# Spectrum rows for the second half of the partitions: copied once within HBM, then read with one load per chunk

## The chip, the cores and the metric

The kernel runs on one core of a Trainium2 chip. The metric is the device time of one execution in microseconds (us); lower is better. A profile of one more execution shows what each engine did: TensorE (PE, with its weight loads as PEld), VectorE (DVE), ScalarE (ACT), GpSimd (POOL), SyncE (SP, which only issues transfers here), and the DMA engines. "L418" means line 418 of the kernel.

## What is computed

A long convolution along the sequence by FFT, then a token-mixing layer on its result:

```python
# x: (8, 5696, 128), h: (5696, 128)
Yf = rfft(x, n=2*S, axis=1) * rfft(h, n=2*S, axis=0)[None]
y  = irfft(Yf, n=2*S, axis=1)[:, :S, :]
theta = y @ w_theta
u   = y + w_tok_r @ (y * cos(theta)) + w_tok_i @ (y * sin(theta))   # over the sequence
out = u + relu(u @ w_ch)
```

The change touches only the first two lines.

## The kernel before

The convolution takes the first 361 us or so, the mixing nearly all the rest. The transform of length 2 x 5696 is done as two factors, 178 x 64. The 8 sequences and 128 channels are handled in eight groups, each of two sequences and 64 channels (`groups`, L493; `dh` is the half of the channels). A group goes through four stages.

- **Stage A** (`stage_a`, L241): 16 chunks of four matmuls (L250), evicted from PSUM to the tile `a` by ScalarE or VectorE (L257, L259).
- **Stage B** (`stage_b`, L400): 12 chunks of up to eight frequencies (`NCK` is 12). TensorE forms the spectrum of x (`f2`, L262, matmuls L270; after the last chunk `warm` extra matmuls L276), ScalarE copies it out of PSUM as `xs` (L416), and VectorE multiplies it by the spectrum of h (L418; L423 for the short last chunk). The product needs both the real and the imaginary rows of h's spectrum, and on the upper 64 partitions those two exchanged. They lie in HBM as `hf_hbm`, and `load` (L404) brings a chunk into the tile `hs` with two transfers, one for partitions 0 to 63 (L408) and one, with the order of the pair reversed, for partitions 64 to 127 (L409). `hs` has four buffers (`LEAD`): a chunk's load is issued four chunks ahead, when the product of an earlier chunk has released its buffer.
- **Stage C** (`stage_c`, L429): the inverse's first half, 16 chunks of 16 matmuls (L438, L439) into a PSUM tile, evicted to the tile `g` (L443 by ScalarE, L445 by VectorE). In all groups but the last, ScalarE takes the chunks with q % 32 == 24, that is chunks 3, 7, 11 and 15.
- **Stage D** (`stage_d`, L463): the inverse's second half, seven chunks of matmuls (L474) with the table `e_t` of cosines and sines, and with `e_neg`, a negated copy of some of its rows (`e_minus`, L397), evicted to `yt` (L478, L480), which is stored to `yt_hbm` (L487).

`woven` (L280) writes two or more lists of such steps interleaved by given positions. The loop over groups (L762 to L788) writes stage C of group g woven with stage A of group g + 1, the first four spectrum loads of group g + 1 and the loads of x for group g + 2 (L777); then stage B of group g + 1 woven with stage D of group g (L785). Group 0's stages A and B stand before the loop (L517 to L533). In the loop's first pass the rest of the table `e_t` is made too (`e_table`, L384: three VectorE instructions L387, L388, L198, then a sine and a cosine on ScalarE, L195 and L202), and `e_minus` is written at the end of the spectrum loads' list, to run on GpSimd.

The spectrum of h is made first (`h_chunk`, L351) and stored to `hf_hbm` by eight transfers (L364), each of three chunks for the real or the imaginary rows.

The x loads (`load_x`, L137) are issued by GpSimd, eight pieces of two transfers (L153). Each piece starts with a one-element copy on GpSimd (L151) that reads an evicted chunk of `g`, so that it isn't issued before that chunk is there; piece i reads chunk 2i.

What sets the order: up to the end of the first pass of the loop (`ordered`, L159 to L779) the instructions of VectorE, ScalarE and GpSimd run as written. TensorE and SyncE, and every engine after that, are put in order by a planner, which goes by the written order but takes what it reckons ready first. Each engine, SyncE among them, then runs its instructions strictly in the planned order.

Of the kernel before, what the change touches and what calls it, by code (L numbers as in the profile page):

```python
# [12 lines left out]
F16 = mybir.dt.float16  # L13
add = mybir.AluOpType.add
mult = mybir.AluOpType.mult
# [7 lines left out]
def kernel(  # L23
# [10 lines left out]
    nc = tc.nc  # L34
    B, S, D = x.shape
    assert D == 128
    P = 128
# [38 lines left out]
    N2 = 64  # L76
    N1 = NF // N2
    NB = S // N2
    K1 = N1 // 2 + 1
    CK = 8  # L80
    HD = D // 2
    EN = N2 // 2 + 1
    WARM = 12
# [4 lines left out]
    NCK = len(CHK)  # L88
# [4 lines left out]
    NP = 14  # L93
# [1 line left out]
    RC = 2 * NP + 2 * ND  # L95
    M0, N0 = S // 4 // N2, S // 4 % N2
    assert S % 4 == 0 and S // 2 == NB // 2 * N2 + N2 // 2 and 2 * NP < N2 // 2
    hf_hbm = nc.dram_tensor("hf_hbm", (NCK, 2, N2, 2, HD * CK), F16, kind="Internal").ap()
    yt_hbm = nc.dram_tensor("yt_hbm", (D, B, S), BF16, kind="Internal").ap()

    psp = ExitStack()
# [92 lines left out]
    def sine(out_, r, sign):  # L194
        nc.scalar.activation(out_, r, AF.Sin, bias=zero_b[:r.shape[0]], scale=-sign * TWO_PI)  # L195
# [45 lines left out]
    def stage_a(lhs, by_dve=(), a_=None, spare=None):  # L241

        st = {}

        def chunk(q):
            if q == 0:
                st["a"] = fa.tile([P, 2 * K1, HD], F16, tag="a", name="a_") if a_ is None else a_
            ps = psum()
            for i in range(4):
                nc.tensor.matmul(ps[:, i // 2, (i % 2) * 2 * K1:(i % 2 + 1) * 2 * K1], lhs(q + i), f1_t[:NB],  # L250
                                 start=True, stop=True)
            if spare is not None:
                idle(ps, *spare)
            a_out = st["a"][:, :, q:q + 4].rearrange("p k (a q) -> p k a q", a=2)
            a_in = ps[:, :, :4 * K1].rearrange("p a (q k) -> p k a q", q=2)
            if q // 4 in by_dve:
                nc.vector.tensor_copy(a_out, a_in)  # L257
            else:
                nc.scalar.activation(a_out, a_in, AF.Copy)  # L259
        return [lambda q=q: chunk(q) for q in range(0, HD, 4)], st  # L260
# [48 lines left out]
    e_flat, e_neg = e_all[:, :EN * 2 * NB], e_all[:, EN * 2 * NB:].rearrange("p (n r m) -> p n r m", r=2, m=NB)  # L309
    e_t = e_flat.rearrange("p (n r m) -> p n r m", r=2, m=NB)  # L310
# [23 lines left out]
    def h_copy(d0):  # L334
# [5 lines left out]
    steps, a_h = stage_a(lambda q: h16[:NB].rearrange("p h n d -> p (h n) d")[:, :, q], (1, 3, 5, 9),  # L340
                         spare=(2, pad, 512 - 4 * K1))
# [9 lines left out]
    def h_chunk(c):  # L351
        c0, ck = CHK[c]
        ps = f2(a_h, c, 0)
        h_ = hst[c // 6][:, c % 6]
        dst = h_[:, :, :, :ck]
        if c in (0, 2, 5, 7, 10):
            nc.vector.tensor_scalar(dst, ps, 16.0 / NF, None, op0=mult)
        else:
            nc.scalar.activation(dst, ps, AF.Copy, scale=16.0 / NF)
        for cc, j in ((0, 0), (NCK - 1, CHK[-1][1] - 1)):  # L360
            if c == cc:
                nc.vector.tensor_scalar(dst[:, :, :, j], dst[:, :, :, j], 0.5, None, op0=mult)
        for ri in range(2 if c % 3 == 2 else 0):
            nc.sync.dma_start(  # L364
                hf_hbm[c - 2:c + 1, :, :, ri, :].rearrange("c h p n -> p (c h) n"),
                hst[c // 6][64 * ri:64 * ri + 64, c % 6 - 2:c % 6 + 1].rearrange("p c h d k -> p (c h) (d k)"))

    r_u = fc.tile([P, P], F16)
# [15 lines left out]
    def e_table(n):  # L384
        n0 = 11 * n
        t, k, r = ((e_y[0], e_f[1], e_y[0]), (e_y[1], e_y[0], e_y[1]), (e_f[2], e_y[1], e_y[0]))[n]
        nc.vector.tensor_scalar(k, t, MAGIC, None, op0=add)  # L387
        nc.vector.scalar_tensor_tensor(r, k, MAGIC, t, op0=ALU.subtract, op1=ALU.subtract)  # L388
        absolute(k, r)

        def curves():
            t3, k3 = (z.rearrange("p (n m) -> p n m", m=NB) for z in (r, k))
            sine(e_t[:K1, n0:n0 + 11, 1, :], t3, -1)
            cosine(e_t[:K1, n0:n0 + 11, 0, :], k3)
        return curves

    def e_minus():  # L397
        nc.gpsimd.tensor_scalar(e_neg[:K1], e_t[:K1, 1:2 * NP:2], -1.0, None, op0=mult)

    def stage_b(a_st, dh, warm=WARM):  # L400

        hs_of = {}

        def load(c):  # L404
            if c >= NCK:
                return
            hs = hs_of[c] = fh.tile([P, 2, HD * CK], F16, tag="hs", name="hs")
            nc.sync.dma_start(hs[:64], hf_hbm[c, dh])  # L408
            nc.sync.dma_start(hs[64:], hf_hbm[c, dh, :, ::-1, :])  # L409

        def chunk(c):
            c0, ck = CHK[c]
            hv = hs_of[c].rearrange("p r (d k) -> p r d k", k=CK)
            ps = f2(a_st, c, warm)
            xs = fs.tile([P, 2, HD, CK], F16, tag="xs", name="xs")
            nc.scalar.activation(xs[:, :, :, :ck], ps, AF.Copy)  # L416
            if ck == CK:
                nc.vector.tensor_tensor(  # L418
                    uv[:, :, :, c0:c0 + ck],
                    xs.rearrange("p e d k -> p e (d k)").unsqueeze(1).to_broadcast([P, 2, 2, HD * CK]),  # L420
                    hv.rearrange("p r d k -> p r (d k)").unsqueeze(2).to_broadcast([P, 2, 2, HD * CK]), op=mult)
            for r in range(2 if ck < CK else 0):
                nc.vector.tensor_tensor(  # L423
                    uv[:, 2 * r:2 * r + 2, :, c0:c0 + ck], xs[:, :, :, :ck],
                    hv[:, r:r + 1, :, :ck].to_broadcast([P, 2, HD, ck]), op=mult)
            load(c + LEAD)
        return [lambda c=c: load(c) for c in range(LEAD)], [lambda c=c: chunk(c) for c in range(NCK)]

    def stage_c(st, last):  # L429

        def chunk(q):
            if q == 0:
                st["g"] = fg.tile([P, 2 * N2, P], F16, tag="g", name="g_")
            ps = psum()
            for i in range(8):
                o = ps[:, i // 4, (i % 4) * P:(i % 4 + 1) * P]
                at = (q + i) * K1
                nc.tensor.matmul(o, u_t[:, at:at + P], r_u, start=True, stop=False)  # L438
                nc.tensor.matmul(o[:, 2 * NP:], v_t[:, at:at + P], r_v, start=False, stop=True)  # L439
            g_out = st["g"][:K1, :, q:q + 8]  # L440
            g_in = ps[:K1].rearrange("p a (q c) -> p c (a q)", q=4)
            if (last and q % 16 == 0) or (not last and q % 32 == 24):
                nc.scalar.activation(g_out, g_in, AF.Copy)  # L443
            else:
                nc.vector.tensor_copy(g_out, g_in)  # L445
        return [lambda q=q: chunk(q) for q in range(0, 2 * HD, 8)]
# [48 lines left out]
    def front(g, by_dve=(), a_=None, spare=None):  # L495
        if g >= len(groups):
            return [], [], []
        bp, dh = groups[g]
        x16 = x16s[g].rearrange("p b n d -> p (b n) d")
        steps, a_st = stage_a(lambda q: x16[:NB, :, q], by_dve, a_, spare)  # L500
        return (steps, *stage_b(a_st, dh, WARM if g else WARM // 2))

    a0, load0, b0 = front(0, (1, 3, 5, 8, 11, 13), a_0, (1, w_t2[:, 2:5].rearrange("p k n -> p (k n)"), 512 - 4 * K1))
    rr = []
# [257 lines left out]
    for g, (bp, dh) in enumerate(groups):  # L762
        st = {}
        last = g + 1 == len(groups)
        a_, load_, b_ = fronts.pop(g + 1) if g + 1 in fronts else front(g + 1)
        if last:
            for _ in range(3):
                steps0.pop(0)()
        now = ([with_load(steps0.pop(0), n < 6) for n in range(9)] if last else [], 0.0, 0.88)
        c_ = stage_c(st, last)  # L770
        if g == 0:
            ec = []
            now = ([lambda: ec.append(e_table(1)), lambda: ec.pop()()] + [lambda: ec.append(e_table(2)), lambda: ec.pop()()],
                   -0.1, 0.6)
        if g == 0:
            load_ = load_ + [e_minus]
        woven((c_, 0.06 if a_ else 0.0, 1.0), (a_, 0.0, 0.88), now, load_, (load_x(g + 2, st), 0.1, 1.02))  # L777
        if g == 0:
            ordered.close()  # L779
        if g + 2 == len(groups):  # L780
            xin.close()
            open_phases()
            load_ya0()
        now = [steps0.pop(0) for _ in range(5)] if last else []
        woven(b_, (stage_d(st, bp, dh, load_ya1 if last else None), 0.08 if b_ else 0.0, 1.1 if b_ else 1.0), now)  # L785
        if g + 2 == len(groups):
            load_ya1(st["yt"], True)
            open_ring()  # L788
# [307 lines left out]
    for i, (k, p, tt, j0, s0, nj) in enumerate(stretches):  # L1096
# [38 lines left out]
        if tt is None:  # L1135
            if p:
                aside(True, False)
            if first_of_pair:
                q = M1 if p else M3
# [20 lines left out]
            if end_of_pair:  # L1160
# [5 lines left out]
                c, c0 = c_last  # L1166
# [161 lines left out]
```

## Time and profile before

| | |
|---|---|
| median of 3 runs | 2072.84 us (2068.34, 2072.84, 2073.09) |
| profiled execution, its own time | 2070.24 us |
| span from first to last instruction | 2068.4 us |
| mean granted TensorE clock | 0.977 |
| TensorE busy | 1972.6 us, 95% of the span |
| VectorE busy | 1544.1 us, 75% |
| GpSimd busy | 975.9 us, 47% |
| ScalarE busy | 640.0 us, 31% |
| transfers `hs<-hf_hbm` (L408, L409) | 192 of 128 KB, median 3.6 us to landing |

How to read the views that follow. A window row has the stretch of time, its length, then for each engine its busy time with the number of instructions, then the TensorE clock that was granted (1.00 is full speed), the mean busy share of the DMA engines and what they moved in GB/s. A timeline row has the start, the duration (of several merged instructions, if x2 or more), engine, line, operation, the tiles written and read with partitions x elements, and in brackets how long the engine was idle before and what ended that. "SPq" rows are SyncE issuing transfers: their duration is the issue, not the transfer. A row of one line's instructions has the number of them, the shortest, median and longest in ns, and the first and last start. Rows of transfers have their number, the size of each and the median time from issue to landing. Tiles named `ps` are PSUM tiles.

### The profile page before, as it was taken

The page shows a single profiled execution, that of the slowest core. Times are in us where ns is not written, and L with a number is a line of the kernel's source. Part 1 is how long each engine was busy: PE and PEld are TensorE (multiplying, and loading weights), DVE is VectorE, ACT ScalarE, POOL GpSimd, SP SyncE. Part 2 cuts the span into 40 slices and gives each one's busy share as a digit, 9 for nine tenths or more (in the row PEclk, how much of TensorE's full clock was granted, in tenths as well). Part 3 has the DMA queues.
Part 4 walks back from the last instruction along what each step waited for, and adds up shares of the span by engine and source line. Part 5 has one row for each costly group of instructions (what it writes and reads, how often), then busy time and mean ns, then how long its engine had stood idle before and what let it go on. Part 6 is the DMA issues. An engine that isn't in the chain of part 4 may idle for free.

```text
span 2068.4 us, 42651 instructions
## 1 busy us (share of the span) xinstructions
PE 1972.6 (95%) x16205; PEld 1097.1 (53%) x16381; DVE 1544.1 (75%) x2805; ACT 640.0 (31%) x936; POOL 975.9 (47%) x1770
## 2 busy tenths in 40 slices
PE   7699999888999999999999998999999999999998
PEld 5588888754444444444444444444444444444444
DVE  7867777656787878787867666877768677777767
ACT  6667877881323232333300000011111111111111
POOL 8432331365435453636475644454454535454450
PEclk9789999999999999999999999999999999999999
DMA  9699996999889898989899899688796978788793
GB/s 154 105 146 157 166 144 178 254 284 220 143 176 180 172 176 163 179 173 176 172 164 162 122 221 251 112 136 145 134 157 122 155 129 153 137 143 150 127 155 87
DMA packets 513759, 335.08 MB, mean 162 GB/s; under 512 B 185432, under 2 KB 470232, under 8 KB 513464
## 3 DMA queue, kind: packets, MB, share of 16 engines
q0 software_dynamic: 322368, 157.47, 60.0%
q1 hardware_dynamic: 185200, 163.33, 27.3%
q10 hardware_dynamic: 5984, 11.54, 1.6%
q8 instruction: 128, 2.10, 0.4%
q14 instruction: 79, 0.64, 0.1%
HBM read 376.39 MB, written 92.49 MB: 227 GB/s over the span
## 4 chain that ended last, share of the span: by engine, by line
PE 63%; DVE 3%; DMA 3%; POOL 2%; issue 2%; ACT 0%; DVEq 0%; ACTq 0%; POOLq 0%
PE m L1265 59%; DMA b<-z_hbm 2%; POOL ring L666 1%; DVE c L1272 1%; PE utp L960 1%; PE v L967 1%; PE m L1269 1%; DVE b L821 1%; DVE wt L880 1%; PE m L1152 1%; PE theta_ps L550 0%; PE tpz L908 0%; DMA ring<-in_moe_w_tok_r_dram 0%; DMA ring<-in_moe_w_tok_i_dram 0%; PE m L1186 0%
## 5 line engine op out<-in xcount | busy, mean ns | idle before, releaser
L666 POOL DMA_DIRECT2D ring<-in_moe_w_tok_i_dram x720 | 389.7, 550 | 655.2 <-DVE wt L880 578.9
L666 POOL DMA_DIRECT2D ring<-in_moe_w_tok_r_dram x720 | 388.3, 553 | 143.1 <-DVE wt L880 84.5
L880 DVE STREAM_TRANSPOSE wt<-ring 128x384 f32<-128x384 f32 (+2 forms) x720 | 359.0, 523 | 123.1 <-PE m L1265 78.6
L1265 PE MATMUL m<-b,wt 128*128 128x512 bf16 x1605 | 386.2, 380 | 3.7 <-DVE wt L880 1.7
L1265 PEld LDWEIGHTS <-wt 128*128 128x128 bf16 x1804 | 176.3, 98 | 219.7 <-DVE wt L880 7.9
L1272 DVE TENSOR_TENSOR c<-c,m 128x512 f32<-128x512 f32 x412 | 265.4, 670 | 0.4 <-PE m L1265 0.4
L962 ACT ACTIVATE ring<-utp 128x512 bf16<-128x512 bf16 x85 | 50.8, 597 | 582.5 <-PE utp L960 582.5
L418 DVE TENSOR_TENSOR uv_t<-xs,hs 128x2048 f16<-128x2048 f16 x88 | 110.6, 1290 | 43.2 <-DMA hs<-hf_hbm 22.8
L438 PE MATMUL ps<-r_u,uv_t 128*128 128x128 f16 x1024 | 116.8, 220 | 6.9 <-ACT g__9008 L443 1.6
L1186 PE MATMUL m<-b,wt 128*128 128x512 bf16 x471 | 111.6, 383 | 5.5 <-DMA b<-zz 3.4
L439 PE MATMUL ps<-r_v,uv_t 128*128 128x100 f16 x1024 | 114.4, 208 | 0.4
L957 ACT ACTIVATE ub<-c 128x512 bf16<-128x512 f32 x88 | 55.1, 628 | 192.0 <-DVE c L1227 113.5
L153 POOL DMA_DIRECT2D x<-in_x_dram x128 | 98.3, 773 | 20.4 <-POOL x L151 14.6
L416 ACT ACTIVATE xs<-ps 128x1024 f16<-128x1024 f32 x96 | 91.7, 972 | 46.3 <-DVE uv_t L418 26.7
L439 PEld LDWEIGHTS <-uv_t 128*128 128x128 f16 x1024 | 100.2, 98 | 9.8 <-issue 7.8
L438 PEld LDWEIGHTS <-uv_t 128*128 128x128 f16 x1024 | 100.3, 98 | 1.1 <-DVE uv_t L423 0.7
L1186 PEld LDWEIGHTS <-wt 128*128 128x128 bf16 x528 | 51.0, 99 | 65.0 <-issue 6.7
L270 PEld LDWEIGHTS <-w_t 64*128 64x128 f16 x3240 | 61.3, 102 | 38.6 <-issue 29.5
L552 ACT ACTIVATE red<-theta_ps,magic 128x512 f32<-128x512 f32 (+1 forms) x46 | 31.6, 687 | 155.8 <-PE theta_ps L550 96.9
L910 ACT ACTIVATE ring<-tpz 128x512 bf16<-128x512 bf16 (+1 forms) x46 | 27.5, 597 | 134.0 <-PE tpz L908 120.2
L250 PE MATMUL ps<-f_t,x 89*128 89x180 f16 x512 | 63.8, 255 | 2.1 <-DVE a L257 1.5
L821 DVE TENSOR_TENSOR b<-b 128x1024 bf16<-128x1024 bf16 x100 | 61.4, 682 | 0.0
(2924 smaller groups left out, 3766.6 us busy)
## 6 DMA issues: line engine op xcount, KB each, us to landing
ring<-in_moe_w_tok_r_dram POOLq DMA_DIRECT2D x352, 96.0 KB, 4.5
ring<-in_moe_w_tok_i_dram POOLq DMA_DIRECT2D x352, 96.0 KB, 4.9
ring<-in_moe_w_tok_r_dram POOLq DMA_DIRECT2D x352, 80.0 KB, 4.5
ring<-in_moe_w_tok_i_dram POOLq DMA_DIRECT2D x352, 80.0 KB, 4.0
hs<-hf_hbm SPq DMA_DIRECT2D x192, 128.0 KB, 3.6
cp_hbm<-c SPq DMA_DIRECT2D x88, 256.0 KB, 2.5
c<-cp_hbm SPq DMA_DIRECT2D x88, 256.0 KB, 4.4
out_dram<-c SPq DMA_DIRECT2D x88, 256.0 KB, 4.5
```

The source lines that it names most:

```text
L153: nc.gpsimd.dma_start(x16[p0:p1, e, n0:n0 + 16, :HD], bass.AP(tensor=src.tensor, offset=src.offset + (p0 * N2 + n0) * D + dh * HD, ap=[[N2 ...
L250: nc.tensor.matmul(ps[:, i // 2, (i % 2) * 2 * K1:(i % 2 + 1) * 2 * K1], lhs(q + i), f1_t[:NB], start=True, stop=True)
L416: nc.scalar.activation(xs[:, :, :, :ck], ps, AF.Copy)
L418: nc.vector.tensor_tensor(uv[:, :, :, c0:c0 + ck], xs.rearrange("p e d k -> p e (d k)").unsqueeze(1).to_broadcast([P, 2, 2, HD * CK]), hv. ...
L438: nc.tensor.matmul(o, u_t[:, at:at + P], r_u, start=True, stop=False)
L439: nc.tensor.matmul(o[:, 2 * NP:], v_t[:, at:at + P], r_v, start=False, stop=True)
L666: nc.gpsimd.dma_start(wb[32 * i:32 * i + 32, :ng, :nj * 64], bass.AP(tensor=a.tensor, offset=a.offset + row0 * S + p * H + i * QR + j0 * 6 ...
L821: return [lambda f=f, x=x: f(*x) for f, x in ((nc.vector.tensor_sub, (bt[M3], b12, b22)), (nc.vector.tensor_sub, (bt[M4], b21, b11)), (nc. ...
L880: nc.vector.transpose(wt.rearrange("p j t r -> p (j t r)").bitcast(F32).rearrange("p (j g t) -> p g j t", j=TJ, g=4)[:, :ng, :nj], wb[:, : ...
L1186: nc.tensor.matmul(ms[n // 2 * 2 + h], a[n][:, j, :, r], bts_of[p][jj][n % 2 * 2 + h][:, r, :], start=(n % 2 == 0 and jj == 0 and r == 0), ...
L1265: nc.tensor.matmul(ms[q], a[q][:, j, :, r], bts[jj][q][:, r, :], start=(jj == 0 and r == 0), stop=(jj == NJ - 1 and r == 1 and q not in left))
L1272: nc.vector.tensor_tensor(c, z, ms[q], op=op)
```

## The change

`hf_hbm` gets 128 rows per chunk and half in place of 64. The eight stores fill the first 64 rows. Four transfers from HBM to HBM (`swap_rows`), issued by SyncE and written at the head of the loop's first pass, fill the other 64 with the real and imaginary rows exchanged. Group 0 loads as before; groups 1 to 7 load a chunk with one transfer of 128 partitions. `e_minus` runs on VectorE, woven into stage C of group 0 behind the last two instructions of the table, and the four steps of the table move up in that stage. ScalarE evicts the chunks of stage C with q % 32 == 16 (chunks 2, 6, 10 and 14).

```diff
-    hf_hbm = nc.dram_tensor("hf_hbm", (NCK, 2, N2, 2, HD * CK), F16, kind="Internal").ap()
+    hf_hbm = nc.dram_tensor("hf_hbm", (NCK, 2, P, 2, HD * CK), F16, kind="Internal").ap()
...
             nc.sync.dma_start(
-                hf_hbm[c - 2:c + 1, :, :, ri, :].rearrange("c h p n -> p (c h) n"),
+                hf_hbm[c - 2:c + 1, :, :64, ri, :].rearrange("c h p n -> p (c h) n"),
...
+    def swap_rows():
+        for c0 in range(0, NCK, NCK // 2):
+            for ri in range(2):
+                dst, src = (hf_hbm[c0:c0 + NCK // 2, :, r0:r0 + 64, r, :].rearrange("c h p n -> (c h) p n")
+                            for r0, r in ((64, ri), (0, 1 - ri)))
+                nc.sync.dma_start(dst, src)
+
     def e_minus():
-        nc.gpsimd.tensor_scalar(e_neg[:K1], e_t[:K1, 1:2 * NP:2], -1.0, None, op0=mult)
+        nc.vector.tensor_scalar(e_neg[:K1], e_t[:K1, 1:2 * NP:2], -1.0, None, op0=mult)

-    def stage_b(a_st, dh, warm=WARM):
+    def stage_b(a_st, dh, warm=WARM, first=False):
...
-            nc.sync.dma_start(hs[:64], hf_hbm[c, dh])
-            nc.sync.dma_start(hs[64:], hf_hbm[c, dh, :, ::-1, :])
+            if first:
+                nc.sync.dma_start(hs[:64], hf_hbm[c, dh, :64])
+                nc.sync.dma_start(hs[64:], hf_hbm[c, dh, :64, ::-1, :])
+            else:
+                nc.sync.dma_start(hs, hf_hbm[c, dh])
...
-            if (last and q % 16 == 0) or (not last and q % 32 == 24):
+            if (last and q % 16 == 0) or (not last and q % 32 == 16):
...
-        return (steps, *stage_b(a_st, dh, WARM if g else WARM // 2))
+        return (steps, *stage_b(a_st, dh, WARM if g else WARM // 2, g == 0))
...
         if g == 0:
             ec = []
-            now = ([lambda: ec.append(e_table(1)), lambda: ec.pop()()] + [lambda: ec.append(e_table(2)), lambda: ec.pop()()],
+            swap_rows()
+            now = ([lambda: ec.append(e_table(1)), lambda: ec.pop()(), lambda: ec.append(e_table(2)), lambda: ec.pop()(),
+                    e_minus],
                    -0.1, 0.6)
-        if g == 0:
-            load_ = load_ + [e_minus]
```

## The prediction

> **What bounds the kernel now.** First the whole program in windows: length, busy time of TensorE, its weight loads, VectorE, ScalarE and GpSimd, then the granted TensorE clock, the DMA share and GB/s.
>
> ```profile
> core 0: us, PE busy (x) PEld busy (x) DVE busy (x) ACT busy (x) POOL busy (x), PEclk, DMA share, GB/s
> ...
> 54.35:361.28 306.93, 274.75 (x6319) 254.24 (x6316) 231.38 (x209) 227.63 (x275) 93.55 (x155) 0.90 0.91 149
> ...
> 590.00:2050.00 1460.00, 1441.36 (x7375) 684.07 (x7520) 1104.61 (x2188) 253.12 (x414) 722.57 (x1333) 1.00 0.87 157
> ```
>
> The long token-mixing part (590 to 2050 us) keeps TensorE busy for 1441 of 1460 us at full clock, and no line of it changes. The change lives in the convolution, 54 to 361 us, where TensorE idles 32 us and its clock averages 0.90. What follows starts from results of the convolution, so I take a microsecond won or lost here as a microsecond at the end. The chain of waits can't confirm this:
>
> ```profile
> PE 63%; DVE 3%; DMA 3%; POOL 2%; issue 2%; ACT 0%; DVEq 0%; ACTq 0%; POOLq 0%
> ```
>
> Its links are 73% of the span, so it reaches back to about 0.27 x 2068 = 558 us only. The second view cuts the convolution by stage. Forward-spectrum stages (B, woven with the inverse's second half D of the group before) alternate with inverse stages (C, woven with the next group's first stage A).
>
> ```profile
> 54.35:71.17 16.82, 11.76 (x199) 8.35 (x195) 14.01 (x14) 12.83 (x15) 0.00 (x0) 0.54 0.57 164
> 71.17:92.16 20.99, 18.35 (x315) 17.82 (x315) 17.80 (x18) 16.54 (x22) 11.53 (x20) 0.96 0.83 75
> 92.16:124.04 31.88, 22.63 (x563) 20.59 (x561) 22.12 (x15) 15.99 (x19) 14.15 (x14) 0.68 0.71 103
> 124.04:142.41 18.37, 18.30 (x324) 17.80 (x322) 13.80 (x14) 14.50 (x20) 8.50 (x16) 1.00 1.31 170
> 142.41:164.60 22.19, 20.05 (x563) 18.06 (x562) 15.85 (x15) 15.99 (x18) 4.83 (x9) 0.85 0.86 152
> ...
> 182.98:203.62 20.64, 18.60 (x563) 16.69 (x561) 15.61 (x15) 16.07 (x18) 4.60 (x8) 0.92 0.87 142
> ...
> 222.21:241.96 19.75, 17.29 (x563) 15.27 (x560) 15.92 (x15) 15.87 (x18) 4.60 (x8) 1.00 0.91 149
> ...
> 260.35:283.01 22.66, 19.93 (x563) 17.94 (x562) 15.94 (x15) 15.66 (x19) 4.60 (x8) 0.85 0.79 136
> ...
> 301.39:320.30 18.91, 16.99 (x563) 15.25 (x562) 15.76 (x15) 15.79 (x18) 1.67 (x3) 1.00 0.73 144
> ...
> 338.74:361.28 22.54, 19.29 (x560) 17.41 (x559) 15.09 (x14) 15.81 (x18) 3.13 (x6) 0.85 0.78 222
> ```
>
> Stage C (the second and fourth rows) is TensorE's: 18.30 of 18.37 us busy. Stage B+D is nobody's: the same 560 matmuls take 18.91 us in group 6 and 31.88 us in group 1, with lower clocks in the longer ones. That spread is what the change can touch.
>
> **The negated table, from GpSimd to VectorE.** Group 1's long stage holds the table's negation.
>
> ```profile
> 94.37 6.55 POOL L398 TENSOR_SCALAR e_t<-e_t 90x2492 f16<-90x2492 f16 x1
> ```
> ```profile
> 94.12 10.65 DVE L418 TENSOR_TENSOR uv_t<-xs,hs 128x2048 f16<-128x2048 f16 x4 [1.21 <-ACT xs L416]
> ```
> ```profile
> 101.35 2.16 ACT L416 ACTIVATE xs<-ps 128x1024 f16<-128x1024 f32 x2 [6.35 <-DVE uv_t L418]
> ```
> ```profile
> L418 DVE TENSOR_TENSOR uv_t<-xs,hs x88: 1212/1222/7136, 54.4 to 360.6; 128x2048 f16<-128x2048 f16 x88
> ```
>
> One product of the 88 takes 7.14 us instead of 1.22, and four take 10.65 us, exactly while GpSimd runs its 6.55 us negation. VectorE stands still for 7.14 - 1.22 = 5.9 us, ScalarE waits 6.35 us for it, TensorE runs dry and its clock falls to a mean of 0.68. The buffers for the next spectrum chunks come free late as well, and the last loads of x stand behind the negation on GpSimd. So more than 5.9 us goes: the other six B+D stages average (22.19 + 20.64 + 19.75 + 22.66 + 18.91 + 22.54) / 6 = 21.1 us, and 31.88 - 21.1 = **-10.8 us** (bounds -5.9, the stall alone, and -13.0, down to 18.91).
>
> The same negation now costs VectorE time in group 0's stage C.
>
> ```profile
> 28.55 0.97 DVE L234 TENSOR_SCALAR w_t<-w_t,sign 128x2880 f16<-128x2880 f16 x1
> ...
> 30.57 0.40 DVE L232 TENSOR_SCALAR w_t<-w_t 128x960 f16<-128x960 f16 x1
> ```
>
> 2492 elements lie between: 0.40 + (2492 - 960) / (2880 - 960) x 0.57 = 0.85 us. That stage has VectorE busy 17.80 of 20.99 us, so little hides it: **+0.9 us**. The sine and cosine that it reads are issued two chunks earlier than before on ScalarE, so a wait for them should be short; bounds 0 (in a gap) and +3.2 us (it uses up all of the stage's VectorE slack, as a wait). Queued behind it on VectorE are stage C's evictions, for which TensorE's PSUM buffers wait.
>
> **Other chunks evicted by ScalarE.** Chunks 2, 6, 10, 14 of 16 in place of 3, 7, 11, 15; the spacing stays.
>
> ```profile
> 140.81 2.35 DVE L445 CAST g__2479<-ps 90x1024 f16<-90x1024 f32 x2 [0.37 <-PE ps L439]
> ```
> ```profile
> 142.41 1.02 ACT L443 ACTIVATE g__2479<-ps 90x1024 f16<-90x1024 f32 x1 [1.33 <-PE ps L439]
> ```
>
> The last chunk now takes VectorE's 1.2 us instead of ScalarE's 1.02, which delays stage D by about 0.2 us; ScalarE is free sooner for the first eviction of B. Seven times between -0.2 and +0.2: **0**, bounds -1.4 and +1.4. Half of GpSimd's one-element copies that release the x loads now wait for ScalarE; those loads are needed a group later.
>
> **One spectrum load per chunk in groups 1 to 7.**
>
> ```profile
> L408 SPq DMA_DIRECT2D hs<-hf_hbm x96: 444/538/1767, 45.6 to 357.6; - x96
> ```
> ```profile
> L409 SPq DMA_DIRECT2D hs<-hf_hbm x96: 573/600/1736, 47.4 to 359.4; - x96
> ```
> ```profile
> DVE uv_t L418 <- DMA hs<-hf_hbm: 22.8, 17, 5.1
> ```
> ```profile
> hs<-hf_hbm SPq DMA_DIRECT2D x192, 128.0 KB, 3.6
> cp_hbm<-c SPq DMA_DIRECT2D x88, 256.0 KB, 2.5
> c<-cp_hbm SPq DMA_DIRECT2D x88, 256.0 KB, 4.4
> ```
>
> Today a chunk needs two issues, 0.54 + 0.60 us, and is complete about 0.54 + 3.6 = 4.1 us after the first. Pieces fall from 64 of 2 KB plus 128 of 1 KB to 128 of 2 KB. VectorE waits 22.8 us for spectrum rows in 17 places. If the loads came in time, each stage of groups 2 to 7 could fall to 18.91: 3.28 + 1.73 + 0.84 + 3.75 + 0 + 3.63 = 13.2 us at most. But the one 256 KB load of the same 128 partitions in the trace lands in 4.4 us, no sooner than the pair (in another part, beside weight loads), and by it nothing is won. I take a little under half, **-6 us**, since the issue and a third of the pieces do go; bounds 0 and -13.
>
> **The four copies.** They move 2 x 6 x 2 x 64 rows x 2 x 1 KB = 3.1 MB in 3072 pieces of 1 KB, HBM to HBM, which the trace doesn't show. The eight stores of the spectrum moved the same bytes in the same pieces.
>
> ```profile
> 30.74 14.76 SPq L364 DMA_DIRECT2D hf_hbm<-uv_t  x8
> ...
> 53.52 0.57 SPq L409 DMA_DIRECT2D hs<-hf_hbm  x1
> 55.60 0.47 SPq L408 DMA_DIRECT2D hs<-hf_hbm  x1
> ```
> ```profile
> hf_hbm<-uv_t SPq DMA_DIRECT2D x8, 384.0 KB, 9.3
> ```
> ```profile
> q1 hardware_dynamic: 2982, 2.95, 47.4%
> ```
>
> From the window 28 to 50 us the last row gives 0.474 x 16 x 22 / 2982 = 56 ns of a DMA engine per piece, so on 16 engines 3072 pieces take 10.8 us: the lower bound. From the first store to 9.3 us after the last issue, 45.50 + 9.3 - 30.74 = 24.1 us: the upper. Between them I take the 14.8 us for which SyncE was held issuing those stores. The Trainium skill, DMA: Bandwidth & Descriptors, "Why a DMA increments its semaphore by 16 and not by 1", says that a copy spreads over the largest number up to 16 that divides both sides' outermost dimension; here that is 12 (six chunks by two halves). By it the lower bound would be an estimated 10.8 x 16 / 12 = 14.4 us, and the sum would not move. No run here shows a copy's engines yet.
>
> What matters more is **when** the copies go. They are written at the head of group 0's stage C (71 us), but SyncE's order is not fixed by hand; only VectorE's, ScalarE's and GpSimd's are.
>
> ```profile
> 101.28 0.47 SPq L408 DMA_DIRECT2D hs<-hf_hbm  x1
> ...
> 123.72 0.60 SPq L409 DMA_DIRECT2D hs<-hf_hbm  x1
> 124.42 5.89 SPq L487 DMA_DIRECT2D yt_hbm<-yt  x8
> ```
>
> Between 101.28 and 123.72 stand eleven load pairs, eight of group 1 and three of group 2, ahead of group 1's output stores, which the program writes first: a ready transfer moves up into a gap. The copies need only the spectrum stores, so I expect them after group 0's first four loads, from 53.52 + 0.57 = 54.1 us, ahead of its fifth to seventh, which wait for buffers. These then stand behind them in SyncE's queue, and VectorE's products behind those.
>
> ```profile
> 54.35 4.74 DVE L418 TENSOR_TENSOR uv_t<-xs,hs 128x2048 f16<-128x2048 f16 x4 [4.70 <-DMA hs<-hf_hbm]
> ...
> 63.15 1.23 DVE L418 TENSOR_TENSOR uv_t<-xs,hs 128x2048 f16<-128x2048 f16 x1 [1.09 <-ACT xs L416]
> ```
>
> The seventh product, at 63.15 us, would get its rows at 54.1 + 14.8 + 1.1 (issue) + 2.8 = 72.8 us, where 2.8 is this row of the window 50 to 72 us:
>
> ```profile
> hs<-hf_hbm SPq DMA_DIRECT2D x27, 128.0 KB, 2.8
> ```
>
> That is **+9.6 us** (bounds: 10.8 us of copying, +5.7; 24.1 us, +19; not moved up, 0).
>
> **The sum.** -10.8 + 0.9 + 0 - 6 + 9.6 = -6.3 us. The profiled execution took 2070.24 us (2068.4 of it the span), so 2064 us; it lies 2.6 us under the median of the three runs, 2072.84, and they spread over 4.8 us, so I leave it there.
>
> **Rivals.**
> - *The copies stay behind group 0's loads.* They would run in stage C, from about 72 us to 87 or, at the upper bound, 96 us; group 1's first product is due at 94.12. Sum: -15.9, with 1 us for late rows: **2055 us**. For it: the program's place. Against it: the three loads that moved up.
> - *The single load lands no sooner.* Then the 6 us fall away and the copies eat the rest: -10.8 + 0.9 + 9.6 = -0.3, **2070 us**. For it: the 4.4 us row; also that some waits in B are for ScalarE, not for rows. Against it: group 6, with the same work in 18.91 us.
> - *Slower: the copies hold group 0's loads for their upper bound.* The delay is the copying time less 5.1 us. It outweighs -15.9 from 21 us of copying on, and -9.9 (no gain from single loads) from 15 us on. At 24.1 us and no gain from single loads: -9.9 + 19 = +9.1, **2079 us**. For it: HBM is read and written at once, and these stores were held for 14.8 us merely in issue. Against it: from 54 to 71 us GpSimd, which issues the x loads, is idle (0.00 in the row above), so the copies have only group 0's rows beside them.
>
> **Chances.** Forecast 0.45, copies in place 0.24, no gain from single loads 0.12, slower 0.19. I count 0.3% (6.2 us) as what can be told from no change. The forecast's own spread (2056 to 2070) is two thirds beyond that: faster 0.31 + 0.23 + 0.01 = 0.55; slower 0.17 + 0.02 + 0.01 = 0.20; within it 0.25. The range runs from between the second case's time and the full gain in single loads, 2052, to the slower case, 2079; the forecast's own is 2056 to 2070.
>
> **What would show it.** Right: no product of group 1 above 1.3 us, its B+D stage near 21 us; SyncE with 84 single loads; four copies issued between 50 and 60 us, and a gap on VectorE before group 0's fifth to seventh product. Wrong: copies at 70 us and group 0 unchanged (then 2055); B+D stages of groups 2 to 7 unchanged (then 2070); or the mixing part longer than 1460 us, which would mean that what follows does not simply shift.

## The result and the profile after

The changed kernel takes 2053.23 us (median of 4 runs, 2048.57 to 2054.88) where the kernel before takes 2072.51 us beside it: a ratio of 0.9908, 95% interval 0.9886 to 0.9929. That is 19.3 us less: 1.2 us inside the range given (2052 to 2079), outside the forecast's own 2056 to 2070, and 10.8 us under the forecast of 2064. It stands beside the first rival, 2055 us, in which the four copies stay behind group 0's loads. The profiled execution took 2052.18 us (span 2050.4) and is read below.

The convolution in windows, kernel before. The stages are cut here at ScalarE's first eviction of stage A and at its first `xs`, in both kernels alike, so the rows differ a little from those of the prediction. After the length come the busy times of TensorE, its weight loads, VectorE, ScalarE and GpSimd, then the granted clock, the DMA share and GB/s.

```profile
70.96:93.08 22.12, 19.48 (x372) 18.91 (x370) 18.75 (x19) 17.66 (x23) 12.45 (x22) 0.96 0.84 75
93.08:124.04 30.96, 21.71 (x505) 19.72 (x500) 21.37 (x14) 15.07 (x19) 13.23 (x12) 0.67 0.70 104
124.04:143.33 19.29, 19.22 (x380) 18.68 (x377) 14.56 (x14) 15.42 (x21) 8.84 (x17) 1.00 1.26 164
```

The same stages, and the later ones that matter, in the kernel after:

```profile
70.07:90.79 20.72, 18.87 (x359) 18.02 (x358) 19.77 (x21) 17.77 (x22) 12.51 (x21) 1.00 1.31 211
90.79:111.64 20.85, 17.14 (x525) 15.13 (x518) 15.74 (x15) 15.10 (x17) 6.67 (x12) 1.00 0.99 149
111.64:130.46 18.82, 18.75 (x364) 18.36 (x363) 14.02 (x14) 15.54 (x22) 8.92 (x18) 1.00 1.27 175
...
206.39:229.26 22.87, 18.97 (x530) 16.96 (x522) 15.93 (x15) 14.81 (x18) 4.36 (x7) 0.85 0.78 138
...
575.00:2032.00 1457.00, 1437.63 (x7360) 682.38 (x7505) 1102.36 (x2182) 252.44 (x413) 716.50 (x1328) 1.00 0.87 157
```

Group 1's B+D stage falls from 30.96 to 20.85 us and its clock rises from 0.67 to 1.00. Stage C of group 0 is 1.4 us shorter although VectorE has an instruction more in it; stage C of the later groups is 0.47 us shorter. One later B+D stage, 22.87 us at a clock of 0.85, is as long as the long ones of before. The mixing part still has TensorE busy for all but 1.3% of the stretch shown.

Two views of VectorE answer to the 7.14 us product and to the cost of the moved negation: the line of the products, then the timeline of stage C of group 0.

```profile
L428 DVE TENSOR_TENSOR uv_t<-xs,hs x88: 1215/1222/1312, 54.7 to 343.5; 128x2048 f16<-128x2048 f16 x88
```
```profile
82.85 0.80 DVE L405 TENSOR_SCALAR e_t<-e_t 90x2492 f16<-90x2492 f16 x1
...
86.28 3.50 DVE L455 CAST g__1411<-ps 90x1024 f16<-90x1024 f32 x3 [0.36 <-PE ps L449]
```

No product is above 1.31 us, and the negation costs 0.80 us where 0.85 was forecast. SyncE's timeline tells where the copies (L402) went:

```profile
53.73 0.87 SPq L402 DMA_DIRECT2D hf_hbm<-hf_hbm  x1
...
67.78 3.37 SPq L402 DMA_DIRECT2D hf_hbm<-hf_hbm  x3
73.72 22.86 SPq L419 DMA_DIRECT2D hs<-hf_hbm  x6
```

One copy of the four moved up to 54 us, as forecast; three went behind group 0's last load. (L416 and L417 are group 0's pairs of loads, L419 the single loads.) VectorE then waited for rows only a little:

```profile
54.69 4.74 DVE L428 TENSOR_TENSOR uv_t<-xs,hs 128x2048 f16<-128x2048 f16 x4 [4.53 <-DMA hs<-hf_hbm]
60.86 2.36 DVE L428 TENSOR_TENSOR uv_t<-xs,hs 128x2048 f16<-128x2048 f16 x2 [1.44 <-DMA hs<-hf_hbm]
```

Group 0's fifth product waits 1.44 us, and its stage B still ends at 70.07 us, 0.9 us earlier than before. The single loads themselves, issue and then landing:

```profile
L419 SPq DMA_DIRECT2D hs<-hf_hbm x84: 319/320/1071, 73.7 to 339.5; - x84
```
```profile
hs<-hf_hbm SPq DMA_DIRECT2D x84, 256.0 KB, 3.4
```

A chunk is complete about 0.32 + 3.4 = 3.7 us after its issue began, where the pair took 4.1 us.

### The profile page after: what moved, and what is told of

Read it like the earlier page. It is cut to its first block, busy times and chain, and to the rows that moved or that the text cites. A ratio compares the mean times of both kernels' runs of the same rounds, so it can differ in the third digit from the quotient of the medians.

```text
span 2050.4 us, 42565 instructions
## 1 busy us (share of the span) xinstructions
PE 1959.6 (96%) x16205; PEld 1086.2 (53%) x16381; DVE 1538.9 (75%) x2806; ACT 639.9 (31%) x936; POOL 965.2 (47%) x1769
## 4 chain that ended last, share of the span: by engine, by line
PE 66%; DVE 3%; DMA 2%; issue 1%; POOL 0%; ACT 0%; DVEq 0%; ACTq 0%; SPq 0%
PE m L1275 62%; DMA b<-z_hbm 1%; DVE c L1282 1%; DVE b L831 1%; PE v L977 1%; PE utp L970 1%; PE m L1279 1%; DVE wt L890 1%; PE theta_ps L560 0%; PE tpz L918 0%; PE m L1162 0%; PE m L1196 0%; POOL ring L676 0%; DMA c<-cp_hbm 0%; DMA wl<-in_moe_w_tok_i_dram 0%
## 5 line engine op out<-in xcount | busy, mean ns | idle before, releaser
L428 DVE TENSOR_TENSOR uv_t<-xs,hs 128x2048 f16<-128x2048 f16 x88 | 104.4, 1224 | 29.9 <-ACT xs L426 18.2
```

The costliest lines, as they stand in the source:

```text
L428: nc.vector.tensor_tensor(uv[:, :, :, c0:c0 + ck], xs.rearrange("p e d k -> p e (d k)").unsqueeze(1).to_broadcast([P, 2, 2, HD * CK]), hv. ...
```

## The experiments

Each ratio is to the kernel before on the same chip, with its 95% interval. The runs fall in three sets: before had a median of 2066.20 us beside e1 to e4, 2070.84 us beside e5 to e8 and 2067.39 us beside e9 to e11. Within a set absolute times can be compared, across sets ratios.

### e1: the table alone

The kernel before, with the negation on VectorE and the table's steps moved as in the change; pairs of loads, no copies, old evictions.

```diff
-        nc.gpsimd.tensor_scalar(e_neg[:K1], e_t[:K1, 1:2 * NP:2], -1.0, None, op0=mult)
+        nc.vector.tensor_scalar(e_neg[:K1], e_t[:K1, 1:2 * NP:2], -1.0, None, op0=mult)
...
-            load_ = load_ + [e_minus]
```

> Only the negated table goes to VectorE, with the four table steps placed as in the changed kernel; pair loads and the old eviction stay. Theory 'lock' (the negation on GpSimd held VectorE for 5.9 us and dragged group 1 with it, and this is most of the gain): no product above 1.4 us, group 1 from its first xs eviction to the next group's first A eviction falls from 30.96 to 20 to 22 us, the whole 10 to 14 us under the kernel before. Theory 'rows' (group 1 was long mainly because its spectrum rows came late, as pairs): that stretch stays above 24 us and the whole gains 7 us or less.

Measured: 2055.25 us, ratio 0.9953 (0.9938 to 0.9969), so 9.7 us (6.4 to 12.8) of 2066.2. The windows of stage C of group 0 and of group 1's B+D:

```profile
69.49:90.68 21.19, 19.17 (x372) 18.79 (x370) 19.63 (x20) 17.65 (x22) 12.67 (x22) 0.97 0.89 85
90.68:113.57 22.89, 18.91 (x505) 16.50 (x500) 15.19 (x14) 14.97 (x19) 7.26 (x11) 0.85 1.01 156
```

B+D falls to 22.89 us, and no product is above 1.31 us. That is most of what 'lock' said, though the stage is 0.9 us above its range and the gain just short of 10 us; 'rows' is out. Stage C does not grow either: VectorE's busy time in it rises by 0.9 us (18.75 to 19.63) and the stage shortens by 0.9 us. The four steps of the table moved too, so this run alone doesn't price the negation; e9 does.

### e2: the evictions alone

```diff
-            if (last and q % 16 == 0) or (not last and q % 32 == 24):
+            if (last and q % 16 == 0) or (not last and q % 32 == 16):
```

> Only the evictions change: ScalarE takes chunks 2, 6, 10, 14 of stage C. Theory 'neutral' (as forecast: only the boundary between stages C and B moves): group lengths, from first A eviction to first A eviction, within 0.3 us of before on average, the whole within 2 us. Theory 'half a microsecond each' (stage C measured 18.82 in place of 19.30 us is a real gain): groups 1 to 6 shorter by 0.5 us each, the whole 3 to 4 us under the kernel before.

Measured: 2064.27 us, ratio 0.9988 (0.9977 to 1.0000), 2.5 us (0 to 4.8). ScalarE's timeline at the end of stage C of group 1, kernel before:

```profile
142.41 1.02 ACT L443 ACTIVATE g__2479<-ps 90x1024 f16<-90x1024 f32 x1 [1.33 <-PE ps L439]
143.33 1.92 ACT L416 ACTIVATE xs<-ps 128x1024 f16<-128x1024 f32 x2
```

and in e2, where the kernel stands 2.2 us ahead of that:

```profile
139.26 1.02 ACT L443 ACTIVATE g__2479<-ps 90x1024 f16<-90x1024 f32 x1 [0.49 <-PE ps L439]
140.63 1.94 ACT L416 ACTIVATE xs<-ps 128x1024 f16<-128x1024 f32 x2 [0.36 <-PE ps L270]
```

Before, the last chunk of C kept ScalarE from the first spectrum chunk of B; now that chunk is VectorE's, and `xs` waits for TensorE only. From the first eviction to the first `xs` is 18.83 us in place of 19.29. In this profile three of the six such stages are that short and three measure 19.06 to 19.36 us; in the changed kernel all six are near 18.8, which gives 2.8 us. The measured time lies between the two theories, and its interval reaches down to zero, so the run doesn't decide between them.

### e3: table and evictions, loads in pairs

e1 and e2 together.

> The changed kernel without the copies and single loads: table on VectorE and new evictions, pair loads in all groups. Theory 'lock': 11 to 15 us under the kernel before, so 3 to 7 us above the changed kernel, and these lie in groups 2 to 7. Theory 'rows': 8 us under the kernel before or less.

Measured: 2053.91 us, ratio 0.9941 (0.9925 to 0.9957). The parts multiply to 0.9953 x 0.9988 = 0.9941, so no sign that they hinder or help one another.

### e4: copies and single loads alone

The changed kernel with the old evictions, and with the negation back on GpSimd at its old place.

> Only the four copies and the single loads: the negation stays on GpSimd, the evictions are the old ones. Theory 'lock': a product of 6 to 7 us remains in group 1, its B+D stage stays at 29 to 32 us, the whole gains 2 to 6 us. Theory 'rows': the whole gains 8 us or more, with group 1 below 26 us.

Measured: 2056.40 us, ratio 0.9958 (0.9943 to 0.9973), 8.7 us (5.6 to 11.8). With e1 and e2 the product is 0.9899, and the whole change was measured at 0.9908 and 0.9906. Neither theory came out whole: the gain is that of 'rows', the long stage that of 'lock'. The slow product is gone here as well (none above 1.31 us), but group 1's B+D is still 29.44 us. GpSimd's negation runs from 94.49 to 101.04 us; VectorE and TensorE in that stage:

```profile
102.41 1.08 DVE L488 CAST yt<-ps 128x890 bf16<-128x890 f32 x1 [9.38 <-PE ps L484]
```
```profile
101.10 3.16 PE L484 MATMUL ps<-e_t,g__1411 90*128 90x89 f16 x40 [5.60 <-POOL e_t L405]
```

Stage D needs the negated table. In this kernel VectorE's first eviction of D stands ahead of its first product, so VectorE waits 9.38 us for stage D, which waits for GpSimd. By plain dependence the same 6.55 us leaves the stage about as long as the product of 7.14 us did before: a wait that takes the place of the one removed. (The profiled execution, 2062.11 us, was the slowest of the seven.)

### e5: the changed kernel again

> The changed kernel once more, beside the next three on one chip. All theories: 0.987 to 0.993 of the kernel before. The three parts alone gave 0.9953, 0.9988 and 0.9958, which multiply to 0.9899; below 0.9899 they help one another, above it they overlap.

Measured: 2052.38 us (2050.47 to 2053.76), ratio 0.9906 (0.9890 to 0.9921). It is what e6 to e8 are compared with.

### e6: all four copies ahead of group 0's fifth load

```diff
     for f in load0:
         f()
+    swap_rows()
...
-            swap_rows()
```

> The changed kernel with the four copies written right behind group 0's first four loads, so that all four stand ahead of the fifth load in SyncE's queue, which is what the prediction took for the changed kernel. Theory 'queue' (rows that stand behind the copies wait for all of their bytes): group 0's seventh product, at 63.5 us in the changed kernel, starts at 69 to 73 us, and the whole is 5 to 10 us above the changed kernel. Theory 'interleaved' (the one copy that moved up cost 1.4 us, and four cost no more than four times that in part beside other work): seventh product before 68 us, the whole 1 to 4 us above the changed kernel.

Measured: 2060.79 us, ratio 0.9951 (0.9932 to 0.9970): 8.4 us above e5. SyncE's timeline, and then VectorE's:

```profile
53.71 5.93 SPq L402 DMA_DIRECT2D hf_hbm<-hf_hbm  x4
59.74 2.56 SPq L416 DMA_DIRECT2D hs<-hf_hbm  x1
```
```profile
68.74 4.74 DVE L428 TENSOR_TENSOR uv_t<-xs,hs 128x2048 f16<-128x2048 f16 x4 [9.54 <-DMA hs<-hf_hbm]
```

This is the prediction's step, made by hand. The four copies are issued one behind the other, the pair behind them is complete at 68.74 us, 15.0 us after the first copy's issue, and VectorE idles for 9.54 us. The seventh product starts near 68.74 + 2 x 1.19 = 71.1 us; 72.8 was forecast for this case. By the semaphore records of the trace the last of the four copies has landed at 67.61 us, 13.9 us after the first one's issue, where 14.8 us of copying were taken. The 'queue' theory holds.

Two windows of this kernel bear on the page that the prediction cited for the copies' engines:

```profile
56.00:58.00 2.00, 1.08 (x21) 0.59 (x22) 1.99 (x3) 1.84 (x2) 0.00 (x0) 0.50 0.76 267
58.00:60.00 2.00, 1.94 (x54) 1.45 (x49) 1.21 (x2) 1.72 (x2) 0.00 (x0) 0.50 0.81 287
```

The copies have these 4 us almost to themselves, and the mean busy share of the 16 engines is 0.76 and 0.81. In the semaphore records, the first copy's semaphore is raised once at 54.95 us and then 12 times, from 58.55 to 59.45 us. The Trainium skill, DMA: Bandwidth & Descriptors, "Why a DMA increments its semaphore by 16 and not by 1", would have 12 of 16 engines at work, by estimate a share of 0.75; the rows and the 12 landings agree with that, though they don't name the engines.

### e7: two loads again, of 64 partitions each

From the copied rows, so that the pieces stay 2 KB and only the number of issues goes back.

```diff
-                nc.sync.dma_start(hs, hf_hbm[c, dh])
+                for r0 in (0, 64):
+                    nc.sync.dma_start(hs[r0:r0 + 64], hf_hbm[c, dh, r0:r0 + 64])
```

> The changed kernel with two loads per chunk again in groups 1 to 7, one per half of the partitions, each of 64 pieces of 2 KB from the copied rows. The copies stay. Theory 'pieces' (the gain of the single loads comes from 128 pieces in place of 192): the same time as the changed kernel within 2 us, VectorE's waits for spectrum rows about 11 us in total. Theory 'issues' (it comes from one transfer in place of two, in issue time and in the number in flight): 3 to 7 us above the changed kernel, waits for spectrum rows above 15 us in total.

Measured: 2053.64 us, ratio 0.9917 (0.9899 to 0.9935), 1.3 us above e5, less than the intervals can part. VectorE's waits for rows between 60 and 350 us (us in all, times, longest) in the kernel before, in e5 and in e7:

```profile
DVE uv_t L418 <- DMA hs<-hf_hbm: 12.1, 14, 2.8
```
```profile
DVE uv_t L428 <- DMA hs<-hf_hbm: 3.4, 4, 1.6
```
```profile
DVE uv_t L429 <- DMA hs<-hf_hbm: 15.0, 13, 3.3
```

With two issues per chunk the waits come back in full, from 3.4 us (6.8 us in the changed kernel's first profile) to 15.0 us, and the time moves by 1.3 us: the waits speak for 'issues', the time for 'pieces'. So the waits for rows are no measure of the gain; that most of them lie beside other work is likely, not shown. The number of issues is not most of what the loads won by, though the intervals leave room for a part of it.

### e8: the x loads earlier

The changed kernel; piece i of the x loads is gated on chunk i of stage C in place of chunk 2i.

```diff
-                nc.gpsimd.tensor_copy(x16[0:1, e, n0, 0:1], g_[0:1, 0, 16 * i:16 * i + 1])
+                nc.gpsimd.tensor_copy(x16[0:1, e, n0, 0:1], g_[0:1, 0, 8 * i:8 * i + 1])
...
-        woven(..., (load_x(g + 2, st), 0.1, 1.02))
+        woven(..., (load_x(g + 2, st), 0.1, 0.6))
```

> The changed kernel with the x loads released by chunks 0 to 7 of stage C in place of 0, 2, ... 14, so that most of their bytes are through before stage B. It is aimed at the gaps of 1.2 to 3.3 us in TensorE's work in stage B, for which the profile shows no releaser ('issue'), and after which the granted clock falls. Theory 'fetch' (TensorE waits there for its own instructions, whose transfers share the DMA engines with the x loads): no such gap above 1 us in groups 1 to 6, the clock stays at 1.00 in their B+D stages, the whole 2 to 6 us under the changed kernel. Theory 'other' (the gap has nothing to do with the x loads): gaps of 1 us and more remain in three or more groups, the whole within 2 us of the changed kernel.

Measured: 2049.66 us (2046.53 to 2050.48), ratio 0.9888 (0.9871 to 0.9905), 2.7 us under e5. It beats both kernels here, though the two intervals overlap. The profile does not say by what: TensorE's stops (see the last section) are not rarer between 70 and 310 us, so 'fetch' has its time and not its gaps. First the sums of TensorE's idle time that ends in "issue" in e5, then in e8:

```profile
PE ps L270 <- issue: 7.0, 7, 1.7
PE ps L484 <- issue: 1.0, 2, 0.5
```
```profile
PE ps L270 <- issue: 9.8, 13, 2.1
PE ps L484 <- issue: 2.5, 5, 1.1
```

### e9: the negation on GpSimd at the new place

```diff
-        nc.vector.tensor_scalar(e_neg[:K1], e_t[:K1, 1:2 * NP:2], -1.0, None, op0=mult)
+        nc.gpsimd.tensor_scalar(e_neg[:K1], e_t[:K1, 1:2 * NP:2], -1.0, None, op0=mult)
```

> The changed kernel with one word different: the negation runs on GpSimd, but at its new, early place, behind the sine in stage C of group 0. It tells the engine from the place. Theory 'port': GpSimd's 6.55 us instruction costs VectorE only where VectorE reads two SBUF operands at once (the products); in stage C of group 0 VectorE only evicts from PSUM and makes the table, so the engine does not matter once the place is early: time within 3 us of the changed kernel, no product above 1.35 us, group 1's B+D stage near 20.9 us, and perhaps group 0's stage C 0.8 us shorter. Theory 'engine': any VectorE instruction is slowed while GpSimd runs its 6.55 us, so stage C of group 0 grows by 4 to 6 us from 20.4 us and the kernel stands 3 to 6 us above the changed one (near 2056 to 2059 if that one stands at 2053).

Measured: 2053.51 us, ratio 0.9931 (0.9913 to 0.9949). GpSimd and VectorE near the end of stage C of group 0:

```profile
84.79 6.55 POOL L405 TENSOR_SCALAR e_t<-e_t 90x2492 f16<-90x2492 f16 x1
```
```profile
86.29 3.50 DVE L455 CAST g__1411<-ps 90x1024 f16<-90x1024 f32 x3 [1.07 <-PE ps L449]
```

The three evictions that run wholly inside GpSimd's 6.55 us take 3.50 us, as in the kernel after, and stage C is as long without VectorE's 0.80 us as with it (20.71 against 20.72 us). On this the 'port' theory is right: GpSimd's instruction stretched VectorE's products, which read two SBUF tiles, and leaves its evictions out of PSUM alone. The Trainium skill, SBUF — State Buffer, "SBUF: two separate sides", says that the two engines share a pair of ports which one holds for a whole instruction, and that a VectorE instruction with two SBUF inputs is among those that need it against a GpSimd instruction that reads SBUF; the 7.14 us product and the 3.50 us evictions both agree. The total stays open: by time the kernel is within 1.2 us of e5, by ratio 0.25% above it. Group 1's B+D was 25.28 us in this one profile, which 'port' had near 20.9. VectorE in that stage:

```profile
106.71 1.23 DVE L428 TENSOR_TENSOR uv_t<-xs,hs 128x2048 f16<-128x2048 f16 x1 [2.42 <-DMA hs<-hf_hbm]
```

The last x loads stand behind the negation on GpSimd: the last of them is issued at 103.73 us, where the kernel after has issued it by 97.7 us. Between 98 and 108 us a spectrum load lands in 5.0 us here and in 3.3 us there (medians), and this product waits 2.42 us for its rows. So the early place spares VectorE, but in this profile it puts x loads beside the spectrum loads of stage B.

### e10: no x loads in groups 2 to 7

```diff
+        if g > 1:
+            x16s[g] = x16s[g - 2]
+            return []
```

> The changed kernel with the loads of x left out for groups 2 to 7 (they use the tiles of groups 0 and 1 again), so those groups are computed from the x of other sequences. It tells whether TensorE's stops at every 128th matmul come from traffic on the DMA engines. Theory 'fetch': TensorE's instructions arrive in blocks of 256 through the same DMA engines, and a block comes late when thousands of small pieces of x are queued with it: without them the stops of 0.4 us and more that end in 'issue' between 60 and 340 us (9 to 12 us in sum in the changed kernel's two profiles) fall below 3 us, each B+D stage of groups 2 to 7 comes to 18.9 us or less, and the kernel to about 2042 to 2046 if the changed one stands at 2053. Theory 'own': the stops belong to TensorE's sequencer itself: they stay at 9 us or so in sum, and the time falls by less than 4 us.

Measured: 2040.45 us (2037.27 to 2043.75), ratio 0.9868 (0.9845 to 0.9892). The window of group 2's B+D, and TensorE's stops between 70 and 310 us:

```profile
128.58:146.17 17.59, 16.39 (x529) 14.70 (x522) 15.81 (x15) 14.77 (x18) 0.00 (x0) 1.00 0.51 150
```
```profile
PE ps L487 <- issue: 1.8, 3, 1.0
PE ps L273 <- issue: 0.8, 2, 0.6
```

The stops fall from 8.0 us (e5; 10.9 in the changed kernel's first profile) to 2.6 us, no B+D stage of groups 2 to 6 is above 18.6 us, each is granted the full clock, and the kernel is 0.38% (7.9 us) under e5 by ratio, 12 us by time. That is on the side of 'fetch'. But GpSimd's part in these stages goes too (0.00 busy), so the run bounds what the x loads cost and does not single out one way in which they cost it.

### e11: the x loads earlier still

Piece i gated on chunk i/2, written into the first third of stage C.

> The changed kernel with the x loads of a group gated on the first half of the chunks that the earlier experiment e8 gated them on (two pieces for each of chunks 0 to 3 of stage C, instead of one for each of 0 to 7) and written into the first third of the stage. It tells whether the gain of e8 (2.7 us under the changed kernel) goes on when x is taken still further out of stage B. Theory 'further': what x still moves during B goes, 1 to 3 us below e8, 2046 to 2048.5. Theory 'spent': in e8 the last x loads already waited for room in GpSimd's own queue and not for a chunk, so that gating earlier moves nothing: within 1.5 us of e8, 2048 to 2051.

Measured: 2049.19 us (2041.79 to 2052.90), ratio 0.9906 (0.9883 to 0.9928). By time it is beside e8, by ratio beside e5; it does not go further, and it doesn't settle e8's gain.

## Why the prediction was right, and where it was wrong

The range held, but the case that the forecast was made for did not come: the copies did not hold group 0's loads. That the time is still inside the range is owed to the rival with the copies in place. The sum was -10.8 + 0.9 + 0 - 6 + 9.6. Term by term:

- **The stall of group 1, -10.8, with +0.9 for the negation on VectorE: right.** Their sum, -9.9, was measured alone as -9.7 us (e1). In the whole change the stage lost 30.96 - 20.85 = 10.1 us. The instruction was right too, 0.80 against 0.85 us, but its cost was put on the path and it fell into a gap: stage C of group 0 is 20.72 us with it and 20.71 without (e9). The lower bound, 0, was the value.
- **The evictions, 0: probably mis-sized.** It is -2.5 us alone, though the interval runs from 0 to 4.8 (e2), and -2.5 again from e1 to e3. Only one half of the argument shows in the length of the stages: the first `xs` comes 0.47 us sooner in each stage C of the changed kernel, while a cost of the later stage D can't be told from the scatter of the B+D stages. If the 2.5 holds, the bounds of -1.4 and +1.4 were too close.
- **The copies, +9.6: this is the step that failed, in its condition and not in its price.** "I expect them after group 0's first four loads" held for one copy of four. With all four put there by hand, e6 cost 8.4 us, so the price of that placement was right. In the changed kernel it was not paid: group 0's stage B ended 0.9 us earlier than before, and group 1's first product, at 93.89 us, waited for no rows.
- **The single loads, -6: right in size, and not shown in its mechanism.** Copies and loads together measure -8.7 us alone (e4) and about -7 on top of the other two parts (0.9906 and 0.9908 against 0.9941 in e3), with the price of the copies near zero. The reason given was that VectorE would wait less for rows; in e7 those waits are back and the time is nearly kept. Where the gain comes from stays open: e7 says that most of it is not the number of issues, and what is left of the prediction's reasons is the pieces of 2 KB for 1 KB, which no run tried alone. The proof that the prediction named, shorter B+D stages in groups 2 to 6, can't be had from single profiles: they sum to 21.27 + 19.72 + 18.83 + 21.74 + 17.99 = 99.55 us before, 98.48 after, 96.33 in e5, and 92.86 in e1, which has the old pairs. From profile to profile that sum scatters by as much as the loads could have moved it; stops of TensorE that fall differently each time (see the last section) are part of that.

The slower rival had the right place and too high a price: with all four copies ahead, the rows behind them came 15 us after the first issue (e6), not 24.1. *No gain from single loads* is ruled out by e4's interval; the load also lands in 3.4 us, not 4.4.

Taking the 9.6 us out of the sum gives -15.9, and with the evictions at -2.5 in place of 0 it is -18.4; measured were -19.3 and, in e5, -18.5. That it is so close is partly luck, since the parts measured alone add to 9.7 + 2.5 + 8.7 = 20.9 us.

**Why only one copy moved up** can be read, though not proved, from the compiled order of SyncE (row, line, transfer, what it waits for; DMAHW0 to 7 are semaphores of SyncE's transfers, DVE is VectorE's):

```
16 L417 DMACopy hs<-hf_hbm 64x2x512 [waits DMAHW7_49]
17 L402 DMACopy hf_hbm<-hf_hbm 12x64x512 [waits DMAHW0_49]
18 L416 DMACopy hs<-hf_hbm 64x1024 [waits DMAHW1_49,DVE_49]
...
34 L402 DMACopy hf_hbm<-hf_hbm 12x64x512 [waits DMAHW1_49]
...
36 L402 DMACopy hf_hbm<-hf_hbm 12x64x512 [waits DMAHW3_49]
```

SyncE's transfers take eight semaphores in turn, 0 to 7, and each waits for the earlier transfer that used its own. The first four pairs of loads fill all eight. The first copy took the first one that came free; the next copies would have had to wait for another, and by then, it seems, the planner reckoned that loads which were written earlier, and so rank higher, were ready. The prediction looked for what a copy depends on in data and left out this second dependence, on room among the transfers in flight. e6 fits it, since copies that are written earlier go all four; but that the planner decided by it was not tried, with more semaphores for one.

**A microsecond won here is not always one at the end.** The prediction took it so. From 70 to 304 us the gain grew to 16 us and at the end it is 18; about 2 us more appear at the entrance of the mixing, between 400 and 560 us. e5 and e8 show that this entrance can take up such differences. Stage D of group 7 starts at 374.07 us in e5,

```profile
374.07 1.22 PE L484 MATMUL ps<-e_t,g__8928 90*128 90x89 f16 x26 [1.40 <-ACT cos L588]
```

and 3.85 us later in e8,

```profile
377.92 1.22 PE L484 MATMUL ps<-e_t,g__8928 90*128 90x89 f16 x26 [1.40 <-ACT cos L588]
```

yet a line of the mixing, with its first and last start at the end of the row, is level in both, e5 first:

```profile
L1240 PE MATMUL m<-yy,ident_bf x4: 379/379/379, 475.1 to 512.9; 128*128 128x512 bf16 x4
```
```profile
L1240 PE MATMUL m<-yy,ident_bf x4: 379/379/379, 475.4 to 513.3; 128*128 128x512 bf16 x4
```

## What to carry to other kernels

Before you cost a transfer that the planner may move up, read in the compiled order where it went, and count the transfers already in flight on its queue: being ready in data was not enough here. When an instruction on GpSimd stretches a two-operand instruction on VectorE, look at its place as well as at its engine: the late place cost about the same by dependence alone (e4), and the early one spared VectorE but put the x loads behind it later (e9). And where one stage's length scatters by several microseconds from profile to profile, judge a part of a change by its timed runs alone, not by that stage.

## What the hardware showed that was not expected

TensorE now and then stops with no other engine to wait for, and the records say that it is out of instructions. Its timeline in the 22.87 us stage of the kernel after; the count of matmuls stands behind the shape:

```profile
210.11 1.02 PE L484 MATMUL ps<-e_t,g__4597 90*128 90x89 f16 x21 [0.21 <-issue]
211.07 0.64 PE L270 MATMUL ps<-a__4584,w_t 64*128 64x64 f16 x32
211.64 1.39 PE L484 MATMUL ps<-e_t,g__4597 90*128 90x89 f16 x30
212.96 0.84 PE L270 MATMUL ps<-a__4584,w_t 64*128 64x64 f16 x45
217.13 0.71 PE L270 MATMUL ps<-a__4584,w_t 64*128 64x64 f16 x19 [3.33 <-issue]
217.77 2.43 PE L484 MATMUL ps<-e_t,g__4597 90*128 90x89 f16 x30
```

Between two stops lie 21 + 32 + 30 + 45 = 128 matmuls, with a weight load each: 256 instructions. After the 3.33 us stop the same 30 matmuls take 2.43 us in place of 1.39, and the whole stage is granted a clock of 0.85; so this stop cost more than its length. Not every one does: a stop of 2.70 us that ends at 258.40 us lies in a B+D stage of 19.70 us at a clock of 1.00. The table of DMA queues (packets, MB, share) has a queue for instructions:

```profile
q8 instruction: 128, 2.10, 0.4%
```

2.10 MB in 128 packets is 16.4 KB each. The profile counts 16381 weight loads; with a matmul each that is 32762 instructions, 256 to a packet. The trace's records of single packets tie the two together: in this kernel every stop of 0.6 us or more inside stage B between 130 and 340 us (seven, 0.7 to 3.3 us long) ends 1.35 to 1.72 us after a packet of that queue has landed. The packet ahead of the 3.33 us stop took 1.08 us, no longer than others, but it started only 4.6 us after the matmul at 210.11 us had opened the block before. The Trainium skill, Advanced Engine Details and Errata, "ISA Cache", says that instructions are cached in lines of 16 KB, 256 instructions; the distance of the stops and the size of the packets agree. It gives no price for a line that comes late: here that is up to 3.3 us, and after some of them a lower clock. That the packets start late because the x loads are ahead of them fits e10, where 8.0 us of stops became 2.6, with the reservation made there. e8 and e11, with the x loads moved earlier, have more stops and not fewer (12.3 and 13.1 us between 70 and 310 us), and it was not shown packet by packet: the cause stays open.
